# Recurrent cross-attention and a GELU MLP on one core: where second-level sums and GpSimd copies stand in the program

## The chip, the cores and the metric

The kernel runs on one core of a Trainium2 chip. Five engines work side by side: TensorE (PE in the profile, its weight loads PEld), VectorE (DVE), ScalarE (ACT), GpSimd (POOL) and SyncE (SP, which here only issues DMAs). Each engine takes its instructions in the order of the program and waits at an instruction until the semaphores it needs have arrived. The metric is the device time of one execution in microseconds (us).

## The reference

```python
# x: (B, H, S, D) = (8, 8, 512, 64), state: (8, 8, 32, 64)
scores = scale * x @ state^T;  a  = softmax(scores);   xread = a  @ state
scores2 = scale * state @ x^T; a2 = softmax(scores2);  sread = a2 @ x
rows = concat([xread, sread], axis=2)        # per batch 512 + 32 rows
h = rows.transpose(0, 2, 1, 3).reshape(4352, 512) @ w_in   # w_in (512, 2048)
out = gelu_exact(h) @ w_out                  # w_out (2048, 512), out (4352, 512) fp32
```

## The kernel before

A batch has 512 token rows, and 8 batches are worked off one behind the other. For the token rows the product of state and w_in is formed first: `p_mm` makes P = state x w_in (2 x 2048 columns per batch, a head on 32 partitions), and `M(k)` makes one 128-row block of h from P and the transposed softmax AT in PSUM, from which ACT writes g = Gelu(h) in bf16. A batch has 16 such blocks; `M(16 * b + m)` is block m of batch b.

The second matmul, g x w_out, is done by one level of Strassen's scheme (the Winograd form) from batch 1 on: g and w_out are cut into quarters, and seven products `X(b, "1")` to `X(b, "7")` of 16 matmuls of 256 columns replace eight. Four of the left operands are sums of quarters of g, made on DVE by `g_sum`; four of the right ones are differences of w_out's quarters, made once by `w_diff`. For batches 2 to 6 product "2" is itself cut a second time: `sub_sums(b)` makes four small sums on DVE (L721, tile gsub), `w_subs` makes four differences of w_out once (L595, tile q_w), and `sub_a` and `sub_b` do seven products of 4 matmuls of 128 columns (28 in all, L727). Between the two halves ACT copies the first result out (qa), after the second half it copies again (qb), and three small adds on DVE make c2, which stands for product "2". Batches 1 and 7 have product "2" undivided.

The order of all instructions is written out by hand. Batches 0 and 1 form a prologue. Then a loop runs over b = 2 to 7, and each pass ("slot b") has eight steps p = 0 to 7 of two M's each. In slot b the M's are those of batch b, the X products those of batch b - 1 (with "2" and "4" of batch b at its end), and the softmax and P those of batch nb = b + 1. What matters for the change is step p = 3 to p = 7 of a slot:

- p = 3: X(b - 1, "7"), then on DVE the two adds c22 and c21 (L666), then `sub_sums(b)`, four operations on the first quarter of g(b).
- p = 5: X(b - 1, "3"), whose last add on DVE (L666, tile oh) frees PSUM bank o2. Then, in even slots, `reads_mm` (L962), which reads the two xo buffers and frees them. Then `p_all(nb)`: p_mm of four column blocks, 32 matmuls at L441, of which the last eight use bank o2 and a buffer of the pool ps_f; the results are copied to P partly by ACT, partly by DVE (three casts, L1002). Then `sub_a(b)`.
- p = 6: two M's, then `sub_b(b)`. p = 7: two M's, then X(b, "4").

The pool ps_f has four PSUM buffers, which M, p_mm, scores and others share; an M can start only when the buffer it gets has been read out. The pool apool has three buffers (tag gsum) for the sums of g.

POOL does the layout copies of x: `rearr(b)` (L225, two copies into x4, for the DMA transpose on SP's queue) and `rearr_ones(b)` (L235, two copies into xo, which `reads_mm` uses two batches at a time). POOL also issues the loads. Its queue is held back by `hold_for(b, m)` (L1016), a copy of one column of g that waits until block m of batch b is there. `load_st(3, B)` on the same queue loads the states of batches 3 to 7, read by `state_prep(3, B)` at the end of the prologue.

In the prologue `atr(1)` transposes the softmax of batch 1 on PE and copies it on DVE (L376), `burst` makes P blocks (casts at L453 on DVE), `srt(1)` transposes the state read of batch 1 (copied on DVE at L419, tile XSR), and `U` finishes the output rows of batch 0, evacuated on DVE at L519.

In slot 7 there is no next batch; `read_out_slot` and `R` do the MLP for the state rows of all batches, and the last products of batch 7 follow behind the loop, up to the 48 matmuls of L5 and L3 (L773).

Of the kernel before, what the change touches and what calls it, by code (L numbers as in the profile page):

```python
# [10 lines left out]
BF16 = mybir.dt.bfloat16  # L11
AF = mybir.ActivationFunctionType
ALU = mybir.AluOpType
# [4 lines left out]
def kernel(  # L18
# [187 lines left out]
    def begin(b):  # L206
        A = Att()
        atts[b] = A
        A.x4 = x4s[b % 2]
        A.xo = xos[b % 2]  # L210
        if b > 0:
            A.xT = att.tile([128, SJ, HC, 128], BF16, name="xT", tag="xT")
# [8 lines left out]
    def rearr(b, ts=(0, 1)):  # L221
        A = atts[b]
        src = xbs[b].rearrange("p (t c) (j d) -> p t c j d", t=2, d=D)
        for t in ts:
            nc.gpsimd.tensor_copy(  # L225
                out=A.x4[:, :, :, 64 * t:64 * t + 64].rearrange("p j c d -> p c j d"),
                in_=src[:, t],
            )

    def rearr_ones(b):  # L230
        A = atts[b]
        eng = nc.vector if b < 2 else nc.gpsimd
        src = xbs[b].rearrange("p (t c) (j d) -> p t c j d", t=2, d=D)
        for t in range(2):
            eng.tensor_copy(  # L235
                out=A.xo[:, :, :, 2 + 64 * t:66 + 64 * t].rearrange("p j c d -> p c j d"),
                in_=src[:, t],
            )
# [124 lines left out]
    def atr(b, ts=(0, 1)):  # L363
        A = atts[b]
        if 0 in ts:
            A.AT = att.tile([128, SJ, 2, 128], BF16, name="AT", tag="AT")
        for t in ts:
            if b == 0:
                ps = ps_o.tile([128, SJ, 128], BF16, name="aT_ps", tag=f"o{turn[0] % 4}")
                turn[0] += 1  # L370
            else:
                ps = ps_f.tile([128, SJ, 128], BF16, name="aT_ps", tag="f")
            for j in range(SJ):
                nc.tensor.transpose(ps[:, j, :], A.a[:, 2 * j + t, :], ident)
            copy = nc.scalar.copy if b == 0 and t == 0 else nc.vector.tensor_copy
            copy(out=A.AT[:, :, t, :], in_=ps)  # L376
# [167 lines left out]
    def mm2_m(b, m):  # L544
        for j in range(SJ):
            if m == 0:
                ops[b, j] = otile([128, d_model], "op")
            nc.tensor.matmul(  # L548
                ops[b, j],
                lhsT=gs[b][:, m, j * 128:(j + 1) * 128],  # L550
                rhs=w_out_bf[:, m, :],
                start=(m == 0),
                stop=(m == MC - 1),
            )
# [8 lines left out]
    def w_diff(name):  # L563
        if name == "5":
            pair = persist.tile([128, 2, MH, NH], BF16, name="ws_56", tag="mix0")
            w_t["5"], w_t["6"] = pair[:, 0], pair[:, 1]
        elif name != "6":
            tag = {"7": "mix1", "4": "mix2"}[name]
            w_t[name] = persist.tile([128, MH, NH], BF16, name=f"ws_{name}", tag=tag)
        x, y = {  # L570
            "5": (b12, b11),
            "6": (b22, w_t.get("5")),
            "7": (b22, b12),
            "4": (b21, w_t.get("6")),
        }[name]
        nc.vector.tensor_tensor(out=w_t[name], in0=x, in1=y, op=ALU.subtract)
# [7 lines left out]
    def w_sub(k, n):  # L584
        return b21[:, MH // 2 * k:MH // 2 * k + MH // 2, QN * n:QN * n + QN]

    def w_subs():
        sub = ALU.subtract
        for i, (x, y) in enumerate((
            (w_sub(1, 1), w_sub(1, 0)),  # L590
            (w_sub(0, 1), q_w[:, 0]),
            (w_sub(0, 1), w_sub(1, 1)),
            (w_sub(0, 0), q_w[:, 1]),
        )):
            nc.vector.tensor_tensor(out=q_w[:, i], in0=x, in1=y, op=sub)  # L595

    def sub_rhs(name):
        if name in "123":
# [113 lines left out]

        return q

    def sub_sums(b):
        t = apool.tile([128, 4, MH // 2, 128], BF16, name="gsub", tag="gsum")
        got = xs[b, "sub"] = {}
        for i, name in enumerate("5673"):
            x, y, op = chain(name, sub_q(b), got)
            got[name] = t[:, i]  # L720
            nc.vector.tensor_tensor(out=t[:, i], in0=x, in1=y, op=op)  # L721

    def sub_mm(b, name, at, start=False):
        lhs = chain(name, sub_q(b), {})[0] if name in "124" else xs[b, "sub"][name]
# [11 lines left out]
    def sub_a(b):  # L736
        xs[b, 0] = otile([128, 4, QN], "xp", 0)
        for at, name in enumerate("2145"):
            sub_mm(b, name, at, at == 0)
        xs[b, "qa"] = cpool.tile([128, 4, QN], FP32, name="qa", tag="s5")  # L740
        nc.scalar.copy(out=xs[b, "qa"], in_=xs[b, 0])
# [273 lines left out]
    def hold_for(b, m):  # L1015
        nc.gpsimd.tensor_copy(out=hold, in_=gs[b][:, m, 0:1])  # L1016


    def M(*ms):
        for m in ms:  # L1020
            mm1(m // MC, m % MC)
# [137 lines left out]
    M(8, 9)  # L1159
    M(10, 11)  # L1160
    mm2_m(0, 8)
    atr(1)
    mm2_m(0, 9)
    burst([(1, 1), (0, 3)])
    w_subs()
    mm2_m(0, 10)
    M(16, 17)
    M(12, 13)
# [1 line left out]
    M(14, 15)  # L1170
    mm2_m(0, 11)
    w_diff("5")
    begin(2)
    rearr(2)
    xtr_dma(2)
    begin(3)
    rearr(3)
    nc.gpsimd.tensor_copy(out=hold, in_=atts[2].xT[:, 0, 0, 0:1])
    load_st(3, B)
    M(18, 19)  # L1180
# [1 line left out]
    burst([(1, 2), (1, 3)])  # L1182
    U(13)
    state_prep(2, 3, ps_o, "o3")
    w_diff("6")
    M(20, 21)
    M(22, 23)
    exp_table()
# [31 lines left out]
    for b in range(2, B):  # L1220
        nb = b + 1
        for p in range(8):
            k = 16 * b + 2 * p
            if p == 1 and nb < B:
                scores(nb, 0)
                scores(nb, 1)
            if p in (2, 3) and nb < B and (b > 2 or p == 2):
                norm(nb, p - 2)
            if p == 3 and nb + 1 < B:
                xtr_dma(nb + 1)  # L1230
            if p == 5 and nb < B:
                atr_dma(nb)
            if nb == B and p < 5:
                read_out_slot(p)
                if p == 4:
                    r_homes()
                    r_sum("56")
                continue
            late = p == 5 and b % 2 and nb < B
            if late:  # L1240
                M(k)
            elif b != 2 or p != 3:
                M(k, k + 1)
            if b == 2 and p == 2:
                M(k + 2, k + 3)
            if b == 2 and p == 1:
                w_diff("7")
            if p < 5 and nb < B:
                if p == 0:
                    g_sum(b - 1, "56")  # L1250
                if p == 2:
                    if b % 2:
                        srts((b - 1, b))
                    g_sum(b - 1, "7")
                if p == 3:
                    g_sum(b - 1, "3")
                if p < 4:
                    X(b - 1, "1657"[p])
                if p == 3:
                    sub_sums(b)  # L1260
                if b == 2 and p == 2:
                    norm(3, 1)
                    for x in [(2, f, p_mm(2, f, ftile)) for f in (2, 3)]:
                        p_copy(*x)
                if p == 1 and b > 2:
                    sr_w("5216"[b - 3])
            if p == 0 and b + 3 < B:
                hold_for(b, 0)
                load_x(4 if b == 2 else b + 3)
            if p == 1 and b == 2:  # L1270
                hold_for(b, 2)
                rearr_ones(3)
            if p == 6 and b == 2:
                hold_for(b, 12)
                load_x(5)
            if p == 0 and nb + 1 < B:
                begin(nb + 1)
                rearr(nb + 1)
            if nb == B:
                if p == 5:  # L1280
                    R("2")
                    r_sum("73")
                    R("4")
                if p == 6:
                    R("1")
                    X(b, "2")
                    R("6")
                    R("5")
                if p == 7:
                    X(b, "4")  # L1290
                continue
            if p == 5:
                X(b - 1, "3")
                if late:
                    M(k + 1)
                reads = (b, nb) if b % 2 == 0 else ()
                rest = p_all(nb, reads)
                if b == 2:
                    rearr_ones(4)
                elif nb + 1 < B:  # L1300
                    rearr_ones(nb + 1)
                sub_a(b)
                for _, f, ps in rest:
                    nc.scalar.copy(out=Ps[nb][:, 0, f * 512:(f + 1) * 512], in_=ps[0])
            if p == 6:
                sub_b(b)
            if p == 7:
                if nb == B - 1:
                    srts(reads)
                X(b, "4")  # L1310
# [43 lines left out]
```

## Time and profile before

| | |
|---|---|
| time, median of 3 runs (lowest to highest) | 203.82 us (203.16 to 203.97) |
| time of the profiled execution | 203.52 us |
| its span, first to last instruction | 201.8 us |
| granted TensorE clock, mean over the span | 1.000 |
| PE: M, 128 x 512 (L506) | 62.1 us busy, 248 matmuls |
| PE: X, 128 x 256 (L647) | 80.3 us busy, 672 matmuls (four groups) |
| DVE: second-level sums (L721), 20 of 128 x 512 | 9.9 us busy, 414 to 1265 ns each |
| DVE: w_subs (L595), 4 of 128 x 512 | 3.4 us busy, 415 to 1258 ns each |
| POOL: rearr (L225) and rearr_ones (L235), 12 copies each | 12.5 and 14.0 us busy |

The span is counted from the first to the last instruction. In the timeline a row gives the start, the length, the engine, the line, the operation with output and inputs, the number of instructions that were merged, and, in brackets, how long the engine sat idle before it and what ended the wait. The length of an instruction counts from the time at which the engine takes it up, so it holds time in which it stands behind another one. The chain of waits is followed back from the last instruction.

### The profile page before, as it was taken

The page shows a single profiled execution, that of the slowest core. Times are in us where ns is not written, and L with a number is a line of the kernel's source. Part 1 is how long each engine was busy: PE and PEld are TensorE (multiplying, and loading weights), DVE is VectorE, ACT ScalarE, POOL GpSimd, SP SyncE. Part 2 cuts the span into 40 slices and gives each one's busy share as a digit, 9 for nine tenths or more (in the row PEclk, how much of TensorE's full clock was granted, in tenths as well). Part 3 has the DMA queues.
Part 4 walks back from the last instruction along what each step waited for, and adds up shares of the span by engine and source line. Part 5 has one row for each costly group of instructions (what it writes and reads, how often), then busy time and mean ns, then how long its engine had stood idle before and what let it go on. Part 6 is the DMA issues. An engine that isn't in the chain of part 4 may idle for free.

```text
span 201.8 us, 5024 instructions
## 1 busy us (share of the span) xinstructions
PE 194.6 (96%) x2095; PEld 134.1 (66%) x2095; DVE 156.5 (78%) x272; ACT 145.2 (72%) x263; POOL 51.5 (26%) x64
## 2 busy tenths in 40 slices
PE   7899999999999899999999999999999999999994
PEld 2434544365767577767776777677776887878893
DVE  2953879889989959994997999849966897960863
ACT  3775578599896599569966998499958778774220
POOL 8963504423409426600603900000000000000000
PEclk9999999999999999999999999999999999999999
DMA  6999999967594939861595116330124010040054
GB/s 194 194 165 203 205 198 203 181 131 140 90 148 84 215 45 166 174 152 59 58 205 165 48 41 120 120 91 5 50 99 112 0 55 0 3 156 0 10 153 156
DMA packets 40567, 23.16 MB, mean 115 GB/s; under 512 B 21856, under 2 KB 39136, under 8 KB 40544
## 3 DMA queue, kind: packets, MB, share of 16 engines
q0 software_dynamic: 13984, 8.10, 29.9%
q1 hardware_dynamic: 25728, 14.22, 28.1%
q10 hardware_dynamic: 832, 0.52, 0.8%
q8 instruction: 16, 0.26, 0.6%
q14 instruction: 7, 0.06, 0.1%
HBM read 17.30 MB, written 8.91 MB: 130 GB/s over the span
## 4 chain that ended last, share of the span: by engine, by line
PE 82%; DVE 6%; DMA 4%; POOL 4%; ACT 2%; issue 1%; POOLq 0%; DVEq 0%
PE xp L647 35%; PE hp L506 25%; PE xp L727 4%; DMA w_in_bf<-in_moe_w_in_dram 4%; PE sp L866 3%; PE op L548 3%; PE rp L932 3%; PE op L532 2%; PE xp L773 2%; POOL w_in_bf L105 2%; PE pt L333 2%; PE p_ps L441 2%; DVE gsub L721 2%; DVE q_w L595 1%; DVE P L453 1%; DVE oh L666 1%
## 5 line engine op out<-in xcount | busy, mean ns | idle before, releaser
L513 ACT ACTIVATE g<-hp 128x512 bf16<-128x512 f32 x124 | 67.0, 612 | 17.4 <-PE hp L506 17.2
L506 PE MATMUL hp<-AT,P 128*128 128x512 bf16 x248 | 62.1, 379 | 0.4 <-DVE XSR L419 0.4
L647 PEld LDWEIGHTS <-gsum 128*128 128x128 bf16 x416 | 40.4, 98 | 8.9 <-issue 0.4
L647 PE MATMUL xp<-ws,gsum 128*128 128x256 bf16 x320 | 38.2, 273 | 0.0
L506 PEld LDWEIGHTS <-P 128*128 128x128 bf16 x248 | 23.0, 98 | 19.7 <-issue 1.3
L647 PEld LDWEIGHTS <-g 128*128 128x128 bf16 x256 | 24.9, 98 | 4.9
L637 DVE TENSOR_TENSOR gsum<-g 128x2048 bf16<-128x2048 bf16 x14 | 17.6, 1255 | 4.6 <-ACT g L513 4.5
L225 POOL COPY x<-xb 128x1024 bf16<-128x1024 bf16 x12 | 12.5, 1074 | 18.5 <-DMA xb<-in_x_dram 18.5
L647 PE MATMUL xp<-w_out_bf,g 128*128 128x256 bf16 x144 | 17.2, 273 | 0.0
L235 POOL COPY xo<-xb 128x1024 bf16<-128x1024 bf16 x12 | 14.0, 1196 | 11.0 <-PE sr L962 11.0
L647 PE MATMUL xp<-ws,g 128*128 128x256 bf16 x112 | 13.4, 273 | 0.0
L548 PE MATMUL op<-w_out_bf,g 128*128 128x512 bf16 x48 | 11.8, 380 | 0.0
L647 PE MATMUL xp<-w_out_bf,gsum 128*128 128x256 bf16 x96 | 11.5, 272 | 0.0
L666 DVE TENSOR_TENSOR oh<-xp,c 128x512 f32<-128x512 f32 x14 | 9.6, 685 | 2.3 <-PE xp L647 2.0
L356 DVE TENSOR_TENSOR a<-e,ics 128x512 bf16<-128x512 bf16 x14 | 10.6, 754 | 0.5
L441 PE MATMUL p_ps<-w_in_bf,sbd 64*32 64x512 bf16 x248 | 9.7, 381 | 1.2 <-DVE oh L666 0.9
L1002 DVE CAST P<-p_ps 128x512 bf16<-128x512 f32 x15 | 9.4, 682 | 1.6 <-PE p_ps L441 1.5
L353 DVE TENSOR_REDUCE cs<-e 128x16 f32<-128x512 bf16 x14 | 9.5, 679 | 0.9 <-ACT e L340 0.9
L666 DVE TENSOR_TENSOR c<-qb 128x256 f32<-128x256 f32 x5 | 2.5, 506 | 9.7 <-ACT qb L749 9.7
L1016 POOL COPY hold<-g 128x1 bf16<-128x1 bf16 x6 | 3.2, 527 | 24.8 <-ACT g L513 24.8
L513 ACT ACT_TABLE_LOAD x7 | 9.0, 1283 | 0.1
L637 DVE TENSOR_TENSOR gsum<-gsum,g 128x2048 bf16<-128x2048 bf16 x7 | 8.6, 1225 | 0.2
(155 smaller groups left out, 304.7 us busy)
## 6 DMA issues: line engine op xcount, KB each, us to landing
out_dram<-oh SPq DMA_DIRECT2D x15, 256.0 KB, 2.8
xb<-in_x_dram POOLq DMA_DIRECT2D x7, 512.0 KB, 7.5
out_dram<-oh SPq DMA_DIRECT2D x6, 512.0 KB, 3.2
w_in_bf<-in_moe_w_in_dram POOLq DMA_DIRECT2D x6, 256.0 KB, 12.0
out_dram<-osb SPq DMA_DIRECT2D x5, 256.0 KB, 3.0
w_out_bf<-in_moe_w_out_dram POOLq DMA_DIRECT2D x4, 256.0 KB, 8.3
w_out_bf<-in_moe_w_out_dram POOLq DMA_DIRECT2D x2, 512.0 KB, 13.1
x0f<-in_x_dram SPq DMA_DIRECT2D x3, 256.0 KB, 3.9
```

The costliest lines, as they stand in the source:

```text
L225: nc.gpsimd.tensor_copy(out=A.x4[:, :, :, 64 * t:64 * t + 64].rearrange("p j c d -> p c j d"), in_=src[:, t],)
L235: eng.tensor_copy(out=A.xo[:, :, :, 2 + 64 * t:66 + 64 * t].rearrange("p j c d -> p c j d"), in_=src[:, t],)
L353: nc.vector.reduce_sum(out=cs, in_=e4, axis=AX.X)
L356: nc.vector.tensor_tensor(out=A.a[:, :, hs].rearrange("p g (c n) -> p g c n", n=NS), in0=e4, in1=ics[:, :, :].to_broadcast((128, G, 2, NS) ...
L441: nc.tensor.matmul(ps[t][32 * c:32 * c + 32, :], lhsT=sbd[64 * t:64 * t + 64, b, c, 32 * t:32 * t + 32], rhs=w_in_bf[64 * t:64 * t + 64, c ...
L506: nc.tensor.matmul(hp, lhsT=Ps[b][:, t, m * 128:(m + 1) * 128], rhs=atts[b].AT[:, :, t, :], start=(t == 0), stop=(t == 1),)
L513: nc.scalar.activation(out=gs[b][:, m, :], in_=hp, func=AF.Gelu)
L548: nc.tensor.matmul(ops[b, j], lhsT=gs[b][:, m, j * 128:(j + 1) * 128], rhs=w_out_bf[:, m, :], start=(m == 0), stop=(m == MC - 1),)
L637: nc.vector.tensor_tensor(out=got[name], in0=x, in1=y, op=op)
L647: nc.tensor.matmul(ps[:, j - js[0], :], lhsT=lhs[:, m, 128 * j:128 * j + 128], rhs=rhs[:, m, :], start=(first and j == js[0] and m == 0), ...
L666: nc.vector.tensor_tensor(out=out, in0=x, in1=y, op=ALU.add)
L1002: copy(out=Ps[b][:, t, f * 512:(f + 1) * 512], in_=ps[t])
```

## The change

- `w_subs` takes the numbers of the differences it is to make. The first two are made ahead of `atr(1)`, the other two behind it; before, all four stood behind the burst.
- `w_diff("6")` directly follows `w_diff("5")`; before, it stood behind `state_prep(2, 3)`.
- `rearr_ones(3)` stands in the prologue (during the work on batch 1), behind `rearr(3)` and ahead of the hold and `load_st(3, B)`; before, it stood in slot 2, step 1, behind a `hold_for(2, 2)`, which goes.
- `sub_sums` takes the names of the sums. In slots 2 to 6 sum "5" stays at p = 3; "6", "7" and "3" are made at p = 5, behind X(b - 1, "3") and ahead of `p_all`.
- In slots 3 and 5 a `hold_for(b, 11)` stands ahead of `rearr_ones(nb + 1)`.
- Batch 7 has the second level too: its four sums at p = 5 of slot 7, `sub_a` and `sub_b` at p = 6 in place of X(7, "2") and its copy.

```diff
@@ -584,15 +584,15 @@
     def w_sub(k, n):
         return b21[:, MH // 2 * k:MH // 2 * k + MH // 2, QN * n:QN * n + QN]
 
-    def w_subs():
-        sub = ALU.subtract
-        for i, (x, y) in enumerate((
-            (w_sub(1, 1), w_sub(1, 0)),
-            (w_sub(0, 1), q_w[:, 0]),
-            (w_sub(0, 1), w_sub(1, 1)),
-            (w_sub(0, 0), q_w[:, 1]),
-        )):
-            nc.vector.tensor_tensor(out=q_w[:, i], in0=x, in1=y, op=sub)
+    def w_subs(which):
+        for i in which:
+            x, y = (
+                (w_sub(1, 1), w_sub(1, 0)),
+                (w_sub(0, 1), q_w[:, 0]),
+                (w_sub(0, 1), w_sub(1, 1)),
+                (w_sub(0, 0), q_w[:, 1]),
+            )[i]
+            nc.vector.tensor_tensor(out=q_w[:, i], in0=x, in1=y, op=ALU.subtract)
 
     def sub_rhs(name):
         if name in "123":
@@ -712,13 +712,15 @@
 
         return q
 
-    def sub_sums(b):
-        t = apool.tile([128, 4, MH // 2, 128], BF16, name="gsub", tag="gsum")
-        got = xs[b, "sub"] = {}
-        for i, name in enumerate("5673"):
+    def sub_sums(b, names):
+        if "5" in names:
+            xs[b, "subs"] = apool.tile([128, 4, MH // 2, 128], BF16, name="gsub", tag="gsum")
+            xs[b, "sub"] = {}
+        got = xs[b, "sub"]
+        for name in names:
             x, y, op = chain(name, sub_q(b), got)
-            got[name] = t[:, i]
-            nc.vector.tensor_tensor(out=t[:, i], in0=x, in1=y, op=op)
+            got[name] = xs[b, "subs"][:, "5673".index(name)]
+            nc.vector.tensor_tensor(out=got[name], in0=x, in1=y, op=op)
 
     def sub_mm(b, name, at, start=False):
         lhs = chain(name, sub_q(b), {})[0] if name in "124" else xs[b, "sub"][name]
@@ -1159,10 +1161,11 @@
     M(8, 9)
     M(10, 11)
     mm2_m(0, 8)
+    w_subs((0, 1))
     atr(1)
+    w_subs((2, 3))
     mm2_m(0, 9)
     burst([(1, 1), (0, 3)])
-    w_subs()
     mm2_m(0, 10)
     M(16, 17)
     M(12, 13)
@@ -1170,11 +1173,13 @@
     M(14, 15)
     mm2_m(0, 11)
     w_diff("5")
+    w_diff("6")
     begin(2)
     rearr(2)
     xtr_dma(2)
     begin(3)
     rearr(3)
+    rearr_ones(3)
     nc.gpsimd.tensor_copy(out=hold, in_=atts[2].xT[:, 0, 0, 0:1])
     load_st(3, B)
     M(18, 19)
@@ -1182,7 +1187,6 @@
     burst([(1, 2), (1, 3)])
     U(13)
     state_prep(2, 3, ps_o, "o3")
-    w_diff("6")
     M(20, 21)
     M(22, 23)
     exp_table()
@@ -1257,7 +1261,7 @@
                 if p < 4:
                     X(b - 1, "1657"[p])
                 if p == 3:
-                    sub_sums(b)
+                    sub_sums(b, "5")
                 if b == 2 and p == 2:
                     norm(3, 1)
                     for x in [(2, f, p_mm(2, f, ftile)) for f in (2, 3)]:
@@ -1267,9 +1271,6 @@
             if p == 0 and b + 3 < B:
                 hold_for(b, 0)
                 load_x(4 if b == 2 else b + 3)
-            if p == 1 and b == 2:
-                hold_for(b, 2)
-                rearr_ones(3)
             if p == 6 and b == 2:
                 hold_for(b, 12)
                 load_x(5)
@@ -1281,10 +1282,12 @@
                     R("2")
                     r_sum("73")
                     R("4")
+                    sub_sums(b, "5673")
                 if p == 6:
                     R("1")
-                    X(b, "2")
+                    sub_a(b)
                     R("6")
+                    sub_b(b)
                     R("5")
                 if p == 7:
                     X(b, "4")
@@ -1293,11 +1296,14 @@
                 X(b - 1, "3")
                 if late:
                     M(k + 1)
+                sub_sums(b, "673")
                 reads = (b, nb) if b % 2 == 0 else ()
                 rest = p_all(nb, reads)
                 if b == 2:
                     rearr_ones(4)
                 elif nb + 1 < B:
+                    if not reads:
+                        hold_for(b, 11)
                     rearr_ones(nb + 1)
                 sub_a(b)
                 for _, f, ps in rest:
```

## The prediction

> **What bounds the kernel now.** I read the page first. All times are us of the one profiled execution, whose span is 201.8 and whose time is 203.52 (1.72 lies around the span); the median of the runs is 203.82, so its scale stands 0.3 above the sum's.
>
> ```profile
> PE 194.6 (96%) x2095; PEld 134.1 (66%) x2095; DVE 156.5 (78%) x272; ACT 145.2 (72%) x263; POOL 51.5 (26%) x64
> ...
> PE 82%; DVE 6%; DMA 4%; POOL 4%; ACT 2%; issue 1%; POOLq 0%; DVEq 0%
> ```
>
> TensorE is the bound: 96% busy at a granted clock of 1.00 in every stage. An edit pays only if it shortens PE's stream or fills a hole in it, and costs only if it opens a hole. So I next looked in the timeline for PE's holes and who ends them. After the start-up there are two, both ended by VectorE (DVE).
>
> ```profile
> 32.38 2.37 POOL L225 COPY x<-xb 128x1024 bf16<-128x1024 bf16 x2 [7.58 <-DMA xb<-in_x_dram]
> 32.59 1.26 DVE L595 TENSOR_TENSOR q_w<-w_out_bf 128x512 bf16<-128x512 bf16 x1
> ...
> 33.77 1.25 DVE L595 TENSOR_TENSOR q_w<-w_out_bf,q_w 128x512 bf16<-128x512 bf16 x1
> ...
> 34.25 1.02 PE L548 MATMUL op<-w_out_bf,g 128*128 128x512 bf16 x4
> ...
> 34.95 0.71 DVE L419 COPY XSR<-srT 128x128 bf16<-128x128 bf16 x1
> ...
> 35.71 1.02 PE L506 MATMUL hp<-AT,P 128*128 128x512 bf16 x4 [0.44 <-DVE XSR L419]
> ```
>
> Two things are to be seen. M(18) starts at 35.71. Eight such matmuls take 1.73 in the chain, 0.216 each, so the last of the four before it starts at 34.90 and M(18) was due at 35.11: the hole is 0.60 (0.44 after the modelled end). And the same L595 instruction that takes 0.41 at 31.80 takes 1.26 beside GpSimd's copies (POOL). I take from these rows a price: a DVE operation with both inputs in SBUF that meets a running POOL copy ends 0.27 after that copy (35.02 against 34.75), and POOL's next copy ends 0.90 after the DVE operation (34.75 against 33.85). Back to back they alternate, at 1.17 a pair.
>
> ```profile
> 64.54 1.17 DVE L721 TENSOR_TENSOR gsub<-g 128x512 bf16<-128x512 bf16 x1
> ...
> 66.36 2.24 POOL L235 COPY xo<-xb 128x1024 bf16<-128x1024 bf16 x2 [0.92 <-PE sr L962]
> 66.42 1.26 DVE L721 TENSOR_TENSOR gsub<-g,gsub 128x512 bf16<-128x512 bf16 x1
> 66.62 0.54 PEld L441 LDWEIGHTS <-sbd 64*32 64x32 bf16 x25
> 66.62 0.84 PE L441 MATMUL p_ps<-w_in_bf,sbd 64*32 64x512 bf16 x24
> ...
> 67.61 0.68 DVE L666 TENSOR_TENSOR oh<-xp,u 128x512 f32<-128x512 f32 x1
> ...
> 68.34 0.41 PE L441 MATMUL p_ps<-w_in_bf,sbd 64*32 64x512 bf16 x8 [0.88 <-DVE oh L666]
> ```
>
> The second hole is in slot 2 (b = 2): the add of X "3" (oh, L666) stands behind four sums, two of them stretched, and PE's last eight p_ps matmuls wait for its bank. From the first p_ps matmul to sub_a PE takes 68.68 - 66.62 = 2.06 here and 110.83 - 109.72 = 1.11 in slot 4: the hole costs 0.95. In slots 3 to 6 the sums cost PE nothing: oh starts there when X "3" is done or 0.2 later, and PE runs on.
>
> **Part by part.** *w_subs split.* DVE ends norm(1,1) at 28.11 and waits for the transposes until 29.11; two subtractions of 0.42 fit into that 1.00. The other two follow the AT copies, which end at 29.86, and end near 30.6, when the P casts start at 30.59. POOL is idle there (its 7.58 wait), so none is stretched. They read rows 0 to 7 of w_out, which PE already used at 25.2. The XSR copy then runs when its transpose is done, by 34.3, and the hole goes: **-0.60**. If a later wait kept PE back, it would be 0. Next late would be the first M of slot 2, whose AT lands 0.2 to 0.3 ahead of use, but its issue moves up with PE.
>
> *w_diff("6") up.* 1.22 of DVE directly behind w_diff("5"), which waits for w_out's last rows (landing 34.9). Both end by 37.3; behind them stands the evacuation of U(12), which would start at 37.04 with PE 0.60 earlier. 0.3 late, its next reader of the bank is state_prep at 38.4: **0**; without that cover 0.3.
>
> *rearr_ones(3) up.* Two copies of 1.02 go before the hold and load_st on POOL. load_st is issued about 0.5 later, landing at 46.9 instead of 46.4, read at 48.6 (48.0 with PE earlier). xtr_dma stands on SP's queue and waits for rearr only. **0**, at most 0.5 if the load were late. In slot 2 the hold and the two copies at 63.41 vanish, so sum "5" is 0.42 instead of 1.17.
>
> *"6", "7", "3" behind oh, slots 2 to 6.* Queued behind them are the three P casts (1.89 in all), and on these wait PE's next M's: p_ps and the M's share four ps_f buffers. M(p = 6) has its second pair, by the order in which the semaphores of the trace free those buffers, behind DVE's *first* cast, and M(p = 7) its second behind the last. Slot 4 decides:
>
> ```profile
> 109.16 0.69 DVE L666 TENSOR_TENSOR oh<-xp,u 128x512 f32<-128x512 f32 x1 [0.45 <-PE xp L647]
> 109.45 2.04 POOL L235 COPY xo<-xb 128x1024 bf16<-128x1024 bf16 x2 [10.04 <-PE sr L962]
> ...
> 110.44 1.89 DVE L1002 CAST P<-p_ps 128x512 bf16<-128x512 f32 x3 [0.58 <-PE p_ps L441]
> ...
> 111.41 2.04 POOL L225 COPY x<-xb 128x1024 bf16<-128x1024 bf16 x2
> 111.72 1.03 PE L506 MATMUL hp<-AT,P 128*128 128x512 bf16 x4
> ```
>
> POOL's four copies run there from 109.45 on without a pause. By the price above "6" ends 0.27 after the first (110.50): 110.77; the second copy at 111.67, "7" at 111.95; the third at 112.85, "3" at 113.12. The casts read PSUM and were not stretched at 110.44, so they end at 113.7, 114.3 and 114.9. The second pair of M(p = 6) was at 112.15 and now waits for 113.76: **+1.6**. If the buffers come round in the other order (that pair behind ACT's cast, 111.75), sub_b waits 0.2 for "3", M(p = 7) 0.1 and 0.8: +1.1. Those are both ends; I take 1.6, because the present order is the one recorded.
>
> Slot 2: oh starts 1.95 after X "3" begins, as in slot 4, and ends at 66.8; PE's 0.95 is won. But "6" ends at 67.7, "7" at 68.9, "3" (POOL is done) at 69.2, the first cast at 69.8. M(p = 6) would start at 68.62; its second pair waits until 69.84, against 70.02 before. What stays is **-0.18**; with the other order -0.5.
>
> Slots 3 and 5: oh at 88.0 to 88.7, the sums from 88.6, each 0.34 behind the last, to 89.7; first cast 90.4, wanted at 91.0. The hold opens 0.13 behind the Gelu that ends at 89.02, inside the sums. If POOL's first copy starts only behind "3": **0**. If ahead of it, "3" ends near 90.7, the first cast at 91.3: +0.35 a slot. Slot 6 has no POOL work: 0.
>
> *Copies held in slots 3 and 5.* Where they ran (80.30 and 113.37) they stretched DVE operations, but no hole of PE stood there: gain 0, and the cost is the one just bounded.
>
> *Second level for batch 7.* X "2" goes out, 28 short matmuls come in.
>
> ```profile
> 91.46 0.67 PE xp L727 x12
> ...
> 182.05 1.75 PE xp L647 x16
> ```
>
> These chain rows give 56 ns a short matmul, so 28 are 1.56, up to 1.72 with sub_a's 1.05: -0.19 to -0.03; I take **-0.15**. DVE's four sums (1.5) and three adds (1.14) lie in its waits of 1.20 and 4.55 there, ACT's extra 0.63 in 1.97. Without that cover g_sum "6", 1.1 ahead of X "6", would be late.
>
> The Trainium skill, "TensorE: Matmul & The Clock Gate", section "Back-to-back issue gap", speaks against this edit: sustained, a 128-column matmul is put at about 81 ns because its weight load counts. By that the level would take an estimated 2.27 and cost 0.5 instead of saving 0.15. The row of 12 in 0.67 decides.
>
> Sum: -0.60 - 0.18 + 1.61 - 0.15 = +0.68 on 203.52, so 204.2; with 0.3 for the median, **204.5**.
>
> **Rivals.** *A, the other buffer order or a shorter stall:* -0.60 - 0.5 + 1.1 - 0.15 = -0.15, 203.7. For it: three sums put DVE's first cast only 0.1 to 0.2 ahead of ACT's third. Against: before, it is the DVE's in all five slots. *B, slower: the held copies meet the sums in slots 3 and 5.* Decided by the 0.6 between first cast and M. One sum stretched costs 0.35 a slot, two (another 0.83) 1.2: +0.7 to +2.4 on the forecast, 205.2 to 206.9, likeliest 205.5. For it: the Gelu and the sums fall together within 0.2. Against: the third sum is asked for before the copy. *C, faster: slot 4's stall does not reach PE*, because POOL's copies start later or the buffers have slack: -0.60 - 0.95 - 0.15 = -1.70, 202.1. Against: the POOL copies start by PE's own reads, 0.3 ahead of the sum.
>
> **Chances.** Forecast 0.42, A 0.14, B 0.26, C 0.18. A measurement of this kernel can tell about 0.5% (1.02) from no change. The forecast spreads over 204.1 to 205.0, and 0.1 of its 0.42 lies above 204.84; A is "same". Slower 0.36, same 0.46, faster 0.18. The range leaves out most of C and B's far end: 202.8 to 205.9.
>
> **What would show it.** Right: no hole before M(18); no wait of p_ps for oh in slot 2; L721 rows of over 1 in slots 2 and 4, and in slot 4 a hole of 1 to 1.6 at an M ended by a cast (L1002). Wrong: three L721 rows of 0.42 in slot 4, or a hole in slots 3 and 5, or sub_a and sub_b of batch 7 above 1.75 together.

## The result

The changed kernel took 204.3 us in the median of 11 runs (204.12 to 205.57); the kernel before, in 11 runs beside it, 203.36 us (203.09 to 203.97). The means differ by 1.04 us (204.52 and 203.48), a ratio of 1.0051 with a 95% interval of 1.0032 to 1.007: about half a per cent slower, at the edge of what a measurement of this kernel can tell from no change. The forecast was 204.5. The profiled execution took 204.2 with a span of 202.3 (before 203.52 and 201.8).

The totals of the page, which stood at 194.6, 156.5 and 51.5 for PE, DVE and POOL before, hardly moved; nothing can be read from them.

```profile
PE 193.9 (96%) x2102; PEld 134.1 (66%) x2107; DVE 157.3 (78%) x279; ACT 145.8 (72%) x264; POOL 49.9 (25%) x65
```

Where PE stands still is seen when the span is cut by stage. The next view gives the busy time of each engine in chosen stretches of the changed kernel; the first number behind the stretch is its length, the second PE's busy time in it.

```profile
31.00:45.00 14.00, 13.95 (x102) 7.18 (x101) 10.10 (x17) 11.77 (x21) 7.02 (x8) 1.00 1.04 179
45.00:62.00 17.00, 17.00 (x164) 11.46 (x163) 15.70 (x23) 14.97 (x27) 6.19 (x7) 1.00 0.62 106
62.00:72.00 10.00, 9.26 (x165) 6.40 (x164) 8.73 (x17) 7.96 (x16) 3.29 (x4) 1.00 0.82 161
...
106.00:116.00 10.00, 8.52 (x162) 6.17 (x161) 8.29 (x17) 7.29 (x15) 4.57 (x4) 1.00 0.44 107
```

Behind the start-up PE loses 0.74 in slot 2 (62 to 72) and 1.48 in slot 4 (106 to 116), and 0.05 from 31 to 45, where the prologue's hole was. In its timeline the four subtractions (L595) now end by 30.31, before the POOL copies begin, XSR is copied as soon as its transpose is done (1.62 of waiting for it), and M(18) starts with nothing ahead of it:

```profile
29.89 0.42 DVE L595 TENSOR_TENSOR q_w<-w_out_bf,q_w 128x512 bf16<-128x512 bf16 x1
...
31.86 2.02 POOL L225 COPY x<-xb 128x1024 bf16<-128x1024 bf16 x2 [7.40 <-DMA xb<-in_x_dram]
...
33.28 0.73 DVE L419 COPY XSR<-srT 128x128 bf16<-128x128 bf16 x1 [1.62 <-PE srT L416]
...
34.85 1.03 PE L506 MATMUL hp<-AT,P 128*128 128x512 bf16 x4
35.56 1.23 DVE L576 TENSOR_TENSOR ws<-w_out_bf,ws 128x2048 bf16<-128x2048 bf16 x1
```

Slot 2 in the same timeline (L723, L964 and L1004 are L721, L962 and L1002 of before):

```profile
65.56 2.22 POOL L235 COPY xo<-xb 128x1024 bf16<-128x1024 bf16 x2 [4.00 <-PE sr L964]
65.76 1.06 PE L441 MATMUL p_ps<-w_in_bf,sbd 64*32 64x512 bf16 x32
65.82 1.07 DVE L723 TENSOR_TENSOR gsub<-gsub,g 128x512 bf16<-128x512 bf16 x1
66.81 1.25 DVE L723 TENSOR_TENSOR gsub<-g 128x512 bf16<-128x512 bf16 x1
66.92 0.61 PE L729 MATMUL xp<-w_out_bf,g 128*128 128x128 bf16 x8
...
67.82 0.59 PE L506 MATMUL hp<-AT,P 128*128 128x512 bf16 x2
67.98 0.41 DVE L723 TENSOR_TENSOR gsub<-g,gsub 128x512 bf16<-128x512 bf16 x1
68.32 1.88 DVE L1004 CAST P<-p_ps 128x512 bf16<-128x512 f32 x3
69.05 0.59 PE L506 MATMUL hp<-AT,P 128*128 128x512 bf16 x2 [0.64 <-DVE P L1004]
```

All 32 p_ps matmuls run in one go and sub_a follows 1.16 behind the first of them, against 2.06 before: 0.90 won. But the second pair of M(p = 6) starts 1.23 behind the first pair; two matmuls take 0.43, so 0.80 is given back to DVE's first cast (L1004). And slot 4:

```profile
108.48 2.22 POOL L235 COPY xo<-xb 128x1024 bf16<-128x1024 bf16 x2 [10.04 <-PE sr L964]
...
108.80 0.99 DVE L723 TENSOR_TENSOR gsub<-gsub,g 128x512 bf16<-128x512 bf16 x1
...
109.28 1.57 ACT L1004 CAST P<-p_ps 128x512 bf16<-128x512 f32 x3
109.72 1.25 DVE L723 TENSOR_TENSOR gsub<-g 128x512 bf16<-128x512 bf16 x1
...
110.65 2.40 POOL L225 COPY x<-xb 128x1024 bf16<-128x1024 bf16 x2
110.81 0.59 PE L506 MATMUL hp<-AT,P 128*128 128x512 bf16 x2
110.90 1.25 DVE L723 TENSOR_TENSOR gsub<-g,gsub 128x512 bf16<-128x512 bf16 x1
...
112.07 1.87 DVE L1004 CAST P<-p_ps 128x512 bf16<-128x512 f32 x3
...
112.80 0.59 PE L506 MATMUL hp<-AT,P 128*128 128x512 bf16 x2 [1.40 <-DVE P L1004]
```

Three sums take turns with the first three of POOL's four copies, so DVE's casts begin at 112.07 instead of behind three sums of 0.4. The pair that waits for the first of them starts 1.99 behind the pair before it: 1.56 lost. ACT's third cast was done at 110.85, so it isn't what that pair waits for. In both slots the pair starts 0.73 behind the start of DVE's first cast (69.05 and 68.32; 112.80 and 112.07), which is the cast's length and 0.1.

To add up, the start of the same PE group is compared in two traces, from landmark to landmark. The table gives what PE gained (-) or lost (+) against the profiled execution before, in the start-up (to 25 us), the rest of the prologue, slot 2, slot 4 and its wake up to slot 5, and behind it, where batch 7's products stand. The rows e1 to e10 are the experiments of the next section. Each row adds up to the difference of the two spans within 0.1.

| kernel | start-up | prologue | slot 2 | slot 4 | end | ratio to before, 95% |
|---|---|---|---|---|---|---|
| changed kernel | -0.21 | -0.65 | -0.11 | +1.62 | -0.15 | 1.0051 [1.0032, 1.007] |
| e1: all sums back at p = 3 | -0.13 | -0.65 | -0.91 | +0.10 | -0.14 | 0.9912 [0.9887, 0.9937] |
| e8: split of the sums alone | -0.23 | -0.13 | -0.18 | +1.63 | 0 | 1.0084 [1.0054, 1.0113] |
| e2: all four copies of slot 4 held | +0.05 | -0.65 | -0.12 | +0.07, then +1.85 | -0.14 | 1.0052 [1.003, 1.0073] |
| e3: rearr(7) held | -0.12 | -0.64 | -0.11 | +0.84 | -0.14 | 0.9997 [0.9971, 1.0024] |
| e5: copies of slot 4 behind the casts | +0.30 | -0.65 | -0.11 | 0 | -0.14 | 0.9951 [0.9927, 0.9976] |
| e4: w_subs split alone | -0.19 | -0.65 | +0.16 | +0.04 | 0 | 0.9976 [0.9944, 1.0008] |
| e9: rearr_ones(3) in the prologue alone | -0.21 | -0.14 | -0.88 | +0.09 | 0 | 0.9967 [0.9941, 0.9993] |
| e7: e1, rearr_ones(3) in slot 2 | +0.32 | -0.65 | +0.21 | +0.10 | -0.15 | 0.9968 [0.9949, 0.9987] |
| e6: e1 without the new holds | -0.20 | -0.64 | -0.86 | +0.06 | -0.15 | 0.991 [0.9884, 0.9935] |
| e10: e1 without batch 7's second level | -0.01 | -0.65 | -0.87 | +0.06 | 0 | 0.9947 [0.9922, 0.9972] |

The start-up column is the spread of single executions: no edit touches that stretch. The 0.04 to 0.10 in slot 4 of kernels without a stall there is not explained; it lies in or just ahead of the p_ps matmuls. The experiments ran on three chips, each beside the kernel before on the same one.

### The profile page after: what moved, and what is told of

It reads as the page before. It is cut to its first block, busy times and chain, and to the rows that moved or that the text cites. A ratio compares the mean times of both kernels' runs of the same rounds, so it can differ in the third digit from the quotient of the medians.

```text
span 202.3 us, 5055 instructions
## 1 busy us (share of the span) xinstructions
PE 193.9 (96%) x2102; PEld 134.1 (66%) x2107; DVE 157.3 (78%) x279; ACT 145.8 (72%) x264; POOL 49.9 (25%) x65
## 4 chain that ended last, share of the span: by engine, by line
PE 83%; DMA 5%; DVE 4%; POOL 4%; ACT 2%; issue 0%; POOLq 0%
PE xp L647 36%; PE hp L506 26%; DMA xb<-in_x_dram 5%; PE xp L729 4%; PE op L548 3%; PE sp L868 3%; PE rp L934 3%; DVE gsub L723 3%; POOL w_in_bf L105 2%; PE op L532 2%; PE xp L775 2%; PE pt L333 2%; PE p_ps L441 1%; POOL sbd L95 1%; DVE oh L666 1%; ACT P L1004 1%
## 5 line engine op out<-in xcount | busy, mean ns | idle before, releaser
L647 PEld LDWEIGHTS <-g 128*128 128x128 bf16 x240 | 23.3, 98 | 4.8
L225 POOL COPY x<-xb 128x1024 bf16<-128x1024 bf16 x12 | 13.0, 1110 | 19.2 <-DMA xb<-in_x_dram 19.2
L235 POOL COPY xo<-xb 128x1024 bf16<-128x1024 bf16 x12 | 12.8, 1093 | 14.2 <-PE sr L964 14.0
L647 PE MATMUL xp<-w_out_bf,g 128*128 128x256 bf16 x128 | 15.3, 273 | 0.0
L666 DVE TENSOR_TENSOR oh<-xp,c 128x512 f32<-128x512 f32 x14 | 9.6, 686 | 4.1 <-PE xp L647 3.9
L548 PE MATMUL op<-w_out_bf,g 128*128 128x512 bf16 x44 | 11.1, 380 | 0.5 <-issue 0.3
L666 DVE TENSOR_TENSOR oh<-xp,u 128x512 f32<-128x512 f32 (+2 forms) x9 | 5.2, 573 | 8.1 <-PE xp L647 7.8
L1004 DVE CAST P<-p_ps 128x512 bf16<-128x512 f32 x15 | 9.4, 680 | 0.0
L666 DVE TENSOR_TENSOR c<-qb 128x256 f32<-128x256 f32 x6 | 2.6, 426 | 8.4 <-ACT qb L751 8.3
L441 PE MATMUL p_ps<-w_in_bf,sbd 64*32 64x512 bf16 x248 | 9.1, 381 | 0.0
```

The lines of the kernel that those rows point to most:

```text
L225: nc.gpsimd.tensor_copy(out=A.x4[:, :, :, 64 * t:64 * t + 64].rearrange("p j c d -> p c j d"), in_=src[:, t],)
L235: eng.tensor_copy(out=A.xo[:, :, :, 2 + 64 * t:66 + 64 * t].rearrange("p j c d -> p c j d"), in_=src[:, t],)
L441: nc.tensor.matmul(ps[t][32 * c:32 * c + 32, :], lhsT=sbd[64 * t:64 * t + 64, b, c, 32 * t:32 * t + 32], rhs=w_in_bf[64 * t:64 * t + 64, c ...
L548: nc.tensor.matmul(ops[b, j], lhsT=gs[b][:, m, j * 128:(j + 1) * 128], rhs=w_out_bf[:, m, :], start=(m == 0), stop=(m == MC - 1),)
L647: nc.tensor.matmul(ps[:, j - js[0], :], lhsT=lhs[:, m, 128 * j:128 * j + 128], rhs=rhs[:, m, :], start=(first and j == js[0] and m == 0), ...
L666: nc.vector.tensor_tensor(out=out, in0=x, in1=y, op=ALU.add)
```

## The experiments

The theory is the recorded sum. The experiments put it against three rivals: that the order alone delays the casts (with no copies involved), that the holds of slots 3 and 5 cost or save something, and that the gains come from other parts than the ones named.

**e1, all four sums at p = 3, the rest of the change kept.**

```diff
                 if p == 3:
-                    sub_sums(b, "5")
+                    sub_sums(b, "5673")
...
-                sub_sums(b, "673")
```

> The changed kernel with all four sums of slots 2 to 6 at p = 3 again, everything else of the change kept (rearr_ones(3) in the prologue, the holds, w_subs, batch 7). Theory (the sums meet POOL's copies in slots 2 and 4 and delay the casts that M waits for): slot 4's stall of 1.56 and slot 2's of 0.81 go, and slot 2 keeps its gain because no copy stands beside the sums at p = 3 any more: about -1.7 us against before, ratio 0.991 to 0.993. Rival 1 (the sums must stand behind oh for slot 2 to gain): the hole of 0.9 in slot 2 comes back, -0.8 us, ratio 0.996. Rival 2 (the held copies of slots 3 and 5 are what costs): still slower than before, ratio 1.002 to 1.005.

202.16 us in the median, ratio 0.9912. Both stalls are gone. The stretches of this kernel's profile, in the columns of above:

```profile
62.00:72.00 10.00, 9.89 (x171) 7.09 (x170) 7.38 (x17) 7.88 (x16) 3.10 (x4) 1.00 0.79 161
...
106.00:116.00 10.00, 9.95 (x174) 7.36 (x172) 7.60 (x16) 7.91 (x17) 3.99 (x4) 1.00 0.37 107
```

PE stands still for 0.11 and 0.05 there. In slot 2 of its timeline the sums are 0.42 each and oh starts at 65.31, before POOL's copy:

```profile
64.98 0.42 DVE L723 TENSOR_TENSOR gsub<-g,gsub 128x512 bf16<-128x512 bf16 x1
...
65.31 0.68 DVE L666 TENSOR_TENSOR oh<-xp,u 128x512 f32<-128x512 f32 x1
65.64 2.03 POOL L235 COPY xo<-xb 128x1024 bf16<-128x1024 bf16 x2 [3.98 <-PE sr L964]
```

So the new place of "6", "7" and "3" costs the change all that its other parts win, and more. Together with e6, this kernel has the lowest ratio measured; its interval lies below 1 and below that of the changed kernel.

**e8, the reverse: the kernel before with the split of the sums alone** (the two functions of the diff that give `sub_sums` a list of names, `sub_sums(b, "5")` at p = 3, `sub_sums(b, "673")` behind X "3").

> The kernel before with the sums split between p = 3 and p = 5 and nothing else. Theory: slot 2 -0.1, slot 4 +1.6 (three sums meet copies), slots 3 and 5 nothing, since their copies run at p = 1: +1.5 us, ratio 1.006 to 1.008. Rival (the split costs only together with the holds or the moved copies): ratio 0.997 to 1.001.

205.82 us and 1.0084. Its interval overlaps that of the changed kernel, which has the gains beside it; by the steps of the table the split alone costs 1.32 and the changed kernel 0.71. M(18) still waits (0.36 idle), slot 2 gives -0.18, slot 4 +1.63. The split does that by itself. The seven runs fall into two groups: three, with the profiled one among them, took 204.63 to 204.87, four 205.82 to 206.05. What the four lose beyond the steps is not shown.

**e2, rearr_ones(6) moved from slot 4's p = 5 to p = 6, behind a hold.** This also holds rearr(7), which stands behind it on POOL's queue.

```diff
+            if p == 6 and b == 4:
+                hold_for(b, 12)
+                rearr_ones(6)
...
-                elif nb + 1 < B:
+                elif nb + 1 < B and b != 4:
```

> The changed kernel with rearr_ones(6) in slot 4 held for block 12 of g(4), so that POOL's four copies start behind the three sums. DVE's order is unchanged. Theory (contention with the copies): the three sums take 0.42 each, the stall of 1.56 at the second pair of M(p = 6) goes to 0 to 0.2, -1.5 us against the changed kernel, ratio to before 0.996 to 0.998. Rival (the order in DVE's queue alone, three sums ahead of the casts): the sums alone put the first cast back by 0.5, a stall of 0.5 or more stays and the kernel gains at most 1.0.

At the disputed place, yes: with no copy running, the same sums in the same order take 0.42, and M(p = 6) runs through.

```profile
109.72 0.42 DVE L723 TENSOR_TENSOR gsub<-g,gsub 128x512 bf16<-128x512 bf16 x1
...
110.06 1.88 DVE L1004 CAST P<-p_ps 128x512 bf16<-128x512 f32 x3
...
111.06 1.03 PE L506 MATMUL hp<-AT,P 128*128 128x512 bf16 x4
...
113.58 2.22 POOL L235 COPY xo<-xb 128x1024 bf16<-128x1024 bf16 x2
...
114.93 1.14 DVE L666 TENSOR_TENSOR c<-c,qa 128x256 f32<-128x256 f32 x1
...
116.11 1.01 DVE L666 TENSOR_TENSOR c<-qa 128x128 f32<-128x128 f32 x1
...
117.04 2.05 DVE L637 TENSOR_TENSOR gsum<-g 128x2048 bf16<-128x2048 bf16 x1
...
121.00 1.25 PE L647 MATMUL xp<-ws,gsum 128*128 128x256 bf16 x10 [1.70 <-DVE oh L666]
```

So the order by itself costs PE nothing here; the copies do. But the time missed the expectation: 204.77 us and 1.0052, no gain. The four copies now meet the adds of c2 (0.42 and 0.29 with no copy beside them, here 1.14 and 1.01) and the large g_sum (1.22, here 2.05), DVE falls behind, and X "6" waits 1.70 for an oh that is late. The wait was moved by 8 us and not removed.

**e3, a dose in between: only rearr(7), the last two copies, is held.**

```diff
                 begin(nb + 1)
+                if b == 5:
+                    hold_for(4, 12)
                 rearr(nb + 1)
```

> The changed kernel with only rearr(7) held for block 12 of g(4); rearr_ones(6) still runs beside the sums of slot 4, so two of the three sums meet a copy and the third does not. Theory: one alternation fewer, sum "3" takes 0.42 instead of 1.25, the stall falls from 1.56 by 0.8 to about 0.75; ratio to before 1.000 to 1.002. Rival (the stall is set by something else than the number of copies met): it stays at 1.56, ratio 1.005, or goes altogether, 0.997.

The ratio is 0.9997 (expected 1.000 to 1.002). Two sums meet copies, the third is free, and the stall is half:

```profile
109.82 1.25 DVE L723 TENSOR_TENSOR gsub<-g 128x512 bf16<-128x512 bf16 x1
...
110.92 0.60 PE L506 MATMUL hp<-AT,P 128*128 128x512 bf16 x2
111.00 0.41 DVE L723 TENSOR_TENSOR gsub<-g,gsub 128x512 bf16<-128x512 bf16 x1
...
111.33 1.87 DVE L1004 CAST P<-p_ps 128x512 bf16<-128x512 f32 x3
...
112.06 0.59 PE L506 MATMUL hp<-AT,P 128*128 128x512 bf16 x2 [0.55 <-DVE P L1004]
```

With four, two and no copies there, and so three, two and no sums that meet one, slot 4 loses 1.62, 0.78 and 0.07 at this place (another 0.06 of e3's 0.84 falls in slot 5). The delay and the stall go together: measured from the first pair of M(p = 6), DVE's first cast starts 1.26 behind it in the changed kernel (112.07 and 110.81), 0.41 behind it in e3 and 1.00 ahead of it in e2. That is 2.26 and 1.41 later than in e2, the pair loses 1.56 and 0.71, and in both cases 0.70 of the delay costs nothing.

**e5, the copies of slot 4 in two free gaps:** rearr_ones(6) behind DVE's last cast of the slot, by a copy on POOL that reads that cast's last column, and rearr(7) at p = 2 of slot 5.

```diff
+            if p == 2 and b == 5:
+                hold_for(b, 3)
+                rearr(7)
             if p == 0 and nb + 1 < B:
                 begin(nb + 1)
-                rearr(nb + 1)
+                if b != 5:
+                    rearr(nb + 1)
...
+                    else:
+                        nc.gpsimd.tensor_copy(out=hold, in_=Ps[nb][:, 1, 2047:2048])
                     rearr_ones(nb + 1)
```

> The changed kernel with rearr_ones(6) in slot 4 held for DVE's last P cast and rearr(7) held for block 3 of g(5): the copies stand neither beside the sums nor, all four in a row, beside the c adds and g_sum as in e2. Theory: both the stall at M(p = 6) (1.56 in the changed kernel) and the new hole of 1.7 in front of X(4, "6") of e2 are gone, slot 2's stall of 0.8 stays: -1.5 us against the changed kernel, ratio 0.997 to 0.998. Rival (any place of the copies costs PE about the same, since DVE has no free stretch of 4 us): a hole of 1 us or more opens elsewhere in slots 4 or 5, ratio 1.001 or more.

Ratio 0.9951, a little below what was expected; slot 4 costs 0 and nothing new opens behind it. The split of the sums can be kept if the copies are put elsewhere, but it still gives back 0.80 in slot 2, and e1 is simpler and, by the steps of the table, 0.70 faster (-1.60 against -0.90).

**e4, the kernel before with w_subs split alone** (`w_subs((0, 1))` ahead of `atr(1)`, `w_subs((2, 3))` behind it).

> The kernel before with w_subs split around atr(1) and nothing else. Theory: the hole before M(18) (0.60) goes and nothing else moves: -0.6 us, ratio 0.997. Rival (a later wait takes the place of the one removed, the landing of AT or xT in front of slot 2 and of scores(3)): 0 to -0.3 us, ratio 0.9985 to 1.000.

Ratio 0.9976, by itself not told apart from 1; the trace shows the step: -0.65 in the prologue, no wait at M(18). Slot 2 keeps its hole: the last eight p_ps matmuls wait 1.03 for oh there (before 0.88), so 0.16 of the gain goes again.

**e9, the kernel before with rearr_ones(3) in the prologue alone.**

```diff
     rearr(3)
+    rearr_ones(3)
...
-            if p == 1 and b == 2:
-                hold_for(b, 2)
-                rearr_ones(3)
```

> The kernel before with one edit: rearr_ones(3) issued directly behind rearr(3) ahead of the main loop and no longer, with its hold, in slot 2. All four sums stay at p = 3. Theory: the hole in slot 2 (0.95 of TensorE) comes from those two held copies alone, since without them only sum 5 to 3 at 0.4 each stand ahead of oh; the first p_ps matmul to sub_a falls from 2.06 to about 1.1, the hole of 0.4 to 0.6 before M(18) stays, and no stall opens in slot 4. Ratio to the kernel before about 0.9955 (0.994 to 0.998). Rival: xo's copies (L235) start 0.3 ahead of oh in slot 2 and hold the sums and oh just as well, or load_st issued 0.5 later delays the prologue: then 0.6 or more of the hole is left, and the ratio is 0.999 or above.

Ratio 0.9967. The four sums stand at p = 3 as before, but none is stretched, oh is done in time, and the p_ps matmuls don't break off:

```profile
65.58 0.42 DVE L721 TENSOR_TENSOR gsub<-g,gsub 128x512 bf16<-128x512 bf16 x1
...
65.91 0.68 DVE L666 TENSOR_TENSOR oh<-xp,u 128x512 f32<-128x512 f32 x1
66.08 2.03 POOL L235 COPY xo<-xb 128x1024 bf16<-128x1024 bf16 x2 [3.82 <-PE sr L962]
...
66.28 1.11 PE L441 MATMUL p_ps<-w_in_bf,sbd 64*32 64x512 bf16 x32
```

oh starts 0.17 ahead of POOL's first copy; that is all the room there is. In the kernel before, the hole came in two steps: the copies of rearr_ones(3), from 63.41 on, stretched sum "5" by 0.75, and so sum "3" came at 66.42, just behind the copies that follow `reads_mm` (66.36), and was stretched by another 0.84. Without the first step the second does not happen.

**e7, e1 with rearr_ones(3) put back into slot 2** behind its hold.

> The kernel of e1 with rearr_ones(3) in slot 2 again, behind its hold. Theory (slot 2's hole comes from copies beside the sums, so the move of rearr_ones(3) is what closes it): sums "5" and "3" are stretched to about 1.2 again, oh is late, the hole of 0.9 to 1.0 before the last p_ps matmuls is back, ratio 0.995 to 0.996. Rival (the moved w_diff or the earlier prologue closed it): as e1, 0.991.

Ratio 0.9968. The hole of slot 2 is back with the first sum (1.17) and the fourth stretched again, and slot 2 is 1.12 worse than in e1 (+0.21 against -0.91):

```profile
66.31 1.26 DVE L723 TENSOR_TENSOR gsub<-g,gsub 128x512 bf16<-128x512 bf16 x1
67.49 0.68 DVE L666 TENSOR_TENSOR oh<-xp,u 128x512 f32<-128x512 f32 x1
...
68.22 0.41 PE L441 MATMUL p_ps<-w_in_bf,sbd 64*32 64x512 bf16 x8 [1.09 <-DVE oh L666]
```

With e9 this names what opens the hole: the two copies that used to stand in slot 2, not the earlier prologue or the moved `w_diff`. Putting sums behind oh also lets p_ps run through (e8 and the changed kernel), but then most of the gain is paid at the casts.

**e6, e1 without the holds of slots 3 and 5.**

```diff
-                    if not reads:
-                        hold_for(b, 11)
                     rearr_ones(nb + 1)
```

> The kernel of e1 without the two holds of slots 3 and 5. Theory (the holds are worth nothing, DVE has cover in both places): as e1, ratio 0.991 to 0.992, within 0.3 us of it. Rival (once the sums are back the copies beside the norm and the gsum of slot 3, and beside srm and c of slot 4, reach PE): 0.5 us or more slower than e1.

202.11 us and 0.991, against 202.16 and 0.9912: the holds are worth nothing here.

**e10, e1 without the second level for batch 7** (X "2" undivided again, no sums for it).

```diff
-                    sub_sums(b, "5673")
...
-                    sub_a(b)
+                    X(b, "2")
                     R("6")
-                    sub_b(b)
```

> The kernel after with all four sums at p = 3 and without the second level for batch 7 (X 2 in one piece of 16 matmuls of 256 columns instead of sub_a and sub_b, no sub_sums for batch 7). Theory: X 2 takes 1.74 to 1.76 of TensorE against 1.58 for the two parts, so the time is 0.16 above that of the kernel with the level and the sums at p = 3 (0.9912 of before): ratio about 0.992, not to be told apart by the time, but the trace from the first matmul of M(p = 6) of slot 7 to TensorE's end is 0.16 longer. Rival: the sums and adds of the second level press on VectorE's path at the end, so that without them the end is no later or earlier: 0.991 or below and a stretch no longer.

202.2 us in the median against e1's 202.16, in separate comparisons (0.9947 and 0.9912, whose intervals overlap), so the time tells nothing of 0.16. The trace does: from the group at L934 before X "2" (179.55 here, 179.43 in e1) to the M behind the last group of L934 (183.92, 183.65) it is 4.37 against 4.22, so the level saves 0.15.

## Why the prediction was right, step by step

The mechanism was right: each step came where it was said and with the wait that was named.

- *w_subs split, -0.60.* Measured -0.65, also alone in e4. The hole that it fills varies from execution to execution: in e8 and e9, where w_subs stands as before, the prologue was 0.13 and 0.14 shorter than in the execution the step was read from, which would make the step 0.51.
- *w_diff("6") up, 0.* Its subtraction ends at 36.79 (35.56 and 1.23), and the evacuation of U(12) on DVE follows at once; PE was busy for 13.95 of the 14.00 from 31 to 45. It wasn't tried alone.
- *rearr_ones(3) up, 0 in the prologue.* No wait for the late states: PE is busy throughout 45 to 62 (17.00 of 17.00).
- *Slot 2, -0.18.* Measured -0.11: 0.90 won (0.95 said), 0.80 given back (0.77 said). e9 shows that the gain comes from the two copies that left, and e1 that without the split it stays whole. The rows of over 1 that were to show it are there in slots 2 and 4.
- *Slot 4, +1.6.* Measured +1.62, +1.63 by the split alone. Its price, one sum for one copy at 1.17 a pair, put the second pair of M(p = 6) at 113.76 on the scale of the execution before; it came at 112.80, with PE 0.97 ahead up to there, so at 113.77 on that scale. e2 and e3 show that the copies make the delay.
- *Slots 3 and 5, 0.* The third sum was asked for first, as taken, and POOL's copy followed it. The prediction had named both orders, and the margins are small: 0.28 in slot 3, shown here, and 0.07 in slot 5 (132.05 and 132.12). That slot 5 went this way too is in part luck.

```profile
88.18 0.25 POOL L1018 COPY hold<-g 128x1 bf16<-128x1 bf16 x1 [7.64 <-ACT g L513]
88.30 0.42 DVE L723 TENSOR_TENSOR gsub<-g,gsub 128x512 bf16<-128x512 bf16 x1
88.58 2.03 POOL L235 COPY xo<-xb 128x1024 bf16<-128x1024 bf16 x2
```

- *Batch 7, -0.15.* Measured -0.15 in the table. The parts of sub_a start at 182.54 and end with the next group at 183.46, those of sub_b go from 184.34 to 185.00: 0.92 and 0.66, 1.58 together, against 1.74 for X "2" before (181.89 to 183.63). One reading of the prediction was wrong without effect: four sums of 1.5 do not fit into a wait of 1.20, and DVE's next add (L666, osb) began 0.19 late (183.00, where PE's lag of 0.65 behind before puts it at 182.81).

```profile
182.54 0.61 PE L729 MATMUL xp<-w_out_bf,g 128*128 128x128 bf16 x8
...
183.46 1.03 PE L934 MATMUL rp<-ws,rs 128*128 128x256 bf16 x8
```

The Trainium skill's figure in "TensorE: Matmul & The Clock Gate", section "Back-to-back issue gap", about 81 ns for a sustained 128-column matmul, is not what these rows show: 28 in 1.58 are 56 ns each.

- *The rivals.* A (the other buffer order) fell: the pair waited for DVE's first cast in both slots, 0.73 behind its start. B fell with slots 3 and 5. C, no stall in slot 4, gave 202.1 as its time; that is what e1 and e6 took, where the stall was taken away.

The steps sum to +0.71 in the table (said +0.68). The medians differ by 0.94 and the means by 1.04, with an interval of 0.65 to 1.42 (0.32% to 0.7% of 203.36), so the sum lies inside it, near its lower end.

That the time came within 0.2 of the forecast is in part luck. The prediction added 0.3 because the median of three runs of the kernel before stood that far above its profiled execution. Over eleven runs the median is 203.36, 0.46 below the 203.82 it started from, and the change cost 0.94 instead of 0.68. The two misses have opposite signs.

## What to carry to other kernels

Before moving work of one engine to a later place, look at what the other engine that works in the same memory (SBUF) does *there*, and how much of the next consumer's slack is left: here three operations of 0.4 cost 1.6 because they were put beside four copies, three of which they met. Price such a meeting by the trace (who ends how long behind whom), count the pairs, and follow the delay to the next buffer that PE needs. Holding the copies back is only a repair if the place they are moved to is free too; e2 paid as much 8 us later.

## What the runs showed of the hardware

- DVE operations with two inputs in SBUF take turns with POOL's copies at every size measured here: the smallest add (128 x 128, fp32) went from 0.29 to 1.01, the largest (128 x 2048, bf16) from 1.22 to 2.05. In the same stretches the casts that read PSUM kept 0.62 each (1.88 for three). The expectation of e2 did not count the small fp32 adds, and e2 missed by it; the trace before already had one, 128 x 256, at 0.83 beside a copy (114.98, where 0.42 is usual).
- Without any edit in it, the start-up of the profiled executions differed by up to 0.55 us (-0.23 to +0.32 against the execution before), more than two of the four steps that moved the time. A difference of two spans is no measure of such a step; the distance between two landmarks behind the start-up is: for the prologue's step it came to 0.64 or 0.65 in all nine kernels with the split of w_subs.
